# The order of the front stage: when the queries' weights are loaded, and what goes ahead of them

## The chip, the cores and the metric

The kernel runs on one core of a Trainium2 chip. A core has five engines that run their own instruction queues in order: TensorE (PE: matmuls, with weight loads shown as PEld), VectorE (DVE), ScalarE (ACT), GpSimd (POOL) and SyncE (SP). In this kernel SP does nothing but issue DMAs, plain ones and transposing ones; the bytes are moved by 16 DMA engines. The engines meet through semaphores.

The metric is the device time of one execution in microseconds (us). Before the change the median of three runs is 395.75 us (395.14 to 397.88).

## The reference

One transformer block over 2048 tokens of width 576, in bfloat16: a pre-norm linear attention ("hedgehog") and a pre-norm MLP, each with its residual.

```
h  = x + A(layernorm(x))          A: qkv = y @ wqkv, 32 heads of 18
h2 = h + B(layernorm(h))          B: layernorm, gelu(y @ w1 + b1) @ w2 + b2, 4608 hidden

phi(t)  = concat(softmax(t @ w_phi), softmax(-(t @ w_phi)))      per head, t = q or k
kv      = sum over tokens of phi(k) v^T,   z = sum of phi(k)
o       = phi(q) kv / (phi(q) z + 1e-6),   then o @ wo
```

No softmax over tokens is taken, so the keys of all tokens must be through before the first query can be combined with `kv`.

## The kernel before

**Tiles.** The 2048 tokens lie as 16 tiles of 128; two tiles make a *pair* p = 0..7, and `i` or `a` = 0, 1 names one tile of it (in `stats`, `centre`, `scale`, `sums`), or a half of the 32 heads (in `key_mm`, `key_exp`, `key_sum`, `value_mm`, `value_ev`). Each pair goes through: `stats` (mean and variance, VectorE), `power` (the inverse root, GpSimd), `scale` (the normalised rows, into one of three buffers `lnb`, number p % 3), a turn (the transpose, so that features lie on partitions), `key_mm` and `value_mm` (TensorE), `key_exp` (ScalarE, two exponentials), `key_sum` (VectorE: the softmax's sums and their inverse), `key_weigh` (GpSimd: the product with the inverse, a quarter of a pair each), and `sums` (TensorE, accumulates `kv`).

**A scale on one engine or the other.** VectorE subtracts the mean and multiplies in one instruction. ScalarE multiplies and adds a bias, and the bias, -mean times the inverse root, is first made by GpSimd in `centre`:

```
if eng is act:
    shifted(dst, src, rs, moments[p][2 + i], i)
else:
    eng.tensor_scalar(dst, src, mv[:, i, 0:1], rs[:, i : i + 1], ALU.subtract, ALU.mult)
```

**A turn.** Pairs 0 and 1 are transposed by TensorE (`turn_x_mm`, `turn_x_ev`); all others by `turn_dma` (L315), one transposing DMA on SP's queue from `lnb` (a region of the tile `shared`) into the pair's `home`.

**The weights.** `w_phi` is folded into the projections: the key weights are transposed by TensorE and folded at the start (`flip`, `fold_k`). The query weights go another way: `load_wq` (L598) brings them in by five DMAs, one for each 128 rows, each row in five pieces of 126 columns; `turn_wq(c)` (L368) transposes chunk c by DMA into `wT`; `fold_mm("q", c)` (L393) multiplies it with `w_phi`; `fold_ev` writes it to `wqp`, and `swap_q` copies halves of it between partitions. `load_wo(half)` (L604) brings in the output projection, 648 KB a half; it is first needed by `residual_mm`, after the attention.

**Banks.** The blocks of `key_mm`, `value_mm`, `query_mm` and of the folds share three PSUM tiles in turn (`two`), so a block can start only when the third block before it has been read, mostly by ScalarE.

**The order.** The program is written as a flat list of such calls, and nothing reorders it: each engine executes its instructions in the order in which the list names them. SP's queue before the change, from the start to the 40th microsecond, is

```
load_wk x3, load_x(2, 4), load_x(4, 8), load_values x4, load_x(8, 12), load_wq,
turn_dma(2), turn_wq(4), load_wo(0), turn_wq(1), turn_dma(3), turn_wq(2),
turn_wq(3), turn_wq(0), turn_dma(4), load_x(12, 16), turn_dma(5)
```

TensorE's blocks in the same stretch: keys of pair 0, values and keys of 0 and 1 mixed, keys of pair 2, `value_mm(1, 0)`, `sums(0, 0)`, `value_mm(2, 0)`, `key_mm(1, 1)`, `value_mm(2, 1)`, then `key_mm(3, 0)`, `value_mm(3, 0)`, `key_mm(3, 1)`, `sums(0, 1)`, `value_mm(3, 1)`, `fold_mm("q", 0)`, and the rest of the folds among the pairs 4 and 5. The queries follow from about 50 us, the combination with `kv` and the output projection from about 75 us, and from 90 us to the end the MLP, with the combination of the later pairs in between.

Of the kernel before, what the change touches and what calls it, by code (L numbers as in the profile page):

```python
# [43 lines left out]
def kernel(  # L44
# [213 lines left out]
    def shift(mv, rs, i):  # L258
        nb = small.tile([P, 1], FP32, name="nb", tag="nb", bufs=6)
        nc.gpsimd.tensor_scalar(  # L260
            nb[:, :], mv[:, i, 0:1], rs[:, i : i + 1], -1.0, ALU.mult, ALU.mult
        )
        return nb

    def shifted(dst, src, rs, nb, i):
        nc.scalar.activation(  # L266
            dst, src, AF.Identity, bias=nb[:, :], scale=rs[:, i : i + 1]
        )

    def chunks(t):  # L270
        return xh[:, t, :].rearrange("p (c k) -> p c k", k=KH)
# [6 lines left out]
    def turned(p):  # L278
        return lnT[p // 2][:, p % 2, :, :]

    def stats(p, i):
        if i == 0:
            moments[p] = [small.tile([P, 2, 2], FP32, name="mv", tag="mv")]
        mv = moments[p][0]
        st = small.tile([P, 2, nc.vector.BN_STATS_DIM], FP32, name="st", tag="st")
        for h in range(2):
            nc.vector.bn_stats(st[:, h, :], xh[:, 2 * p + i, h * HALF : (h + 1) * HALF])
        nc.vector.bn_aggr(mv[:, i, :], st[:, :, :])
        if i:
            moments[p] = [mv, None, None, None]  # L290

    def power(p):
        va = small.tile([P, 2], FP32, name="va", tag="va")
        nc.gpsimd.tensor_scalar(va[:, :], moments[p][0][:, :, 1], 1.0, EPS, ALU.mult, ALU.add)
        rs = small.tile([P, 2], FP32, name="rs", tag="rs")
        nc.gpsimd.tensor_tensor(rs[:, :], va[:, :], mhalf[:, 0:2], ALU.pow)
        moments[p][1] = rs

    def centre(p, i):
        moments[p][2 + i] = shift(*moments[p][:2], i)  # L300

    def scale(p, i, eng):
        mv, rs = moments[p][:2]
        dst, src = lnb[p % 3][:, :, i, :], chunks(2 * p + i)
# [3 lines that stand above are left out]
            eng.tensor_scalar(  # L308
                dst, src, mv[:, i, 0:1], rs[:, i : i + 1], ALU.subtract, ALU.mult
            )  # L310

    pool, vec, syn, sca = nc.gpsimd, nc.vector, nc.sync, nc.scalar

    def turn_dma(p):
        nc.sync.dma_start_transpose(  # L315
            turned(p), lnb[p % 3][:, :, :, :].rearrange("p c a k -> p (c a k)")
        )

    act, dve, gps = nc.scalar.copy, nc.vector.tensor_copy, nc.gpsimd.tensor_copy
# [22 lines left out]
    def turn_x_ev(p, part, copy):  # L342
        turned_back(("x", p), turned(p), part, copy)
# [23 lines left out]
    def turn_wq(c):  # L367
        nc.sync.dma_start_transpose(wT[:, :, c * P : (c + 1) * P], wq[:, c, :])  # L368
# [3 lines left out]
    def fold_k_mm(c):  # L372
        flight["k", c] = two.tile([P, 2, 512], FP32, name="pW", tag="two")[:, :, :]
        for g in range(NG):
            k = P if g < NG - 1 else 72
            for a in range(2):
                nc.tensor.matmul(
                    folded_part(g, "k", c, slice(a * KH, (a + 1) * KH)),
                    wT[:k, g, c * KH : (c + 1) * KH],
                    bd[:k, g, 0 : GH[g], :].rearrange("p h f -> p (h f)"),  # L380
                    start=True, stop=True,
                )

    def fold_k_ev(c, copy):
        fold_order.append(c)
        copy(wkp[:, c, :], folded_whole("k", c, P))  # L386
# [30 lines left out]
    def project(dst, lhs, w, i, order):  # L417
        for n, pick in enumerate(order):
            for a in range(2):
                rows = slice(a * KH, (a + 1) * KH)  # L420
                c = pick[a]
                slot = pick[0] if order is CROSSED else c
                nc.tensor.matmul(  # L423
                    dst[:, a, 0:HALF], lhs[rows, c, :], w[rows, slot, i * HALF : (i + 1) * HALF],
                    start=(n == 0), stop=(n == KC - 1),
                )

    def value_mm(p, i):
        pv = flight["v", p, i] = two.tile([P, 2, 512], FP32, name="pv", tag="two")
        project(pv, turned(p), wv, i, PLAIN)  # L430

    def value_ev(p, i, copy):
        copy(
            vals[:, 2 * p : 2 * p + 2, i * HH : (i + 1) * HH, 0:DH],
            flight["v", p, i][:, :, 0:HALF].rearrange("p a (h d) -> p a h d", d=DH),
        )
# [5 lines left out]
    def exponentials(key, dst, p, i):  # L442
        rows = dst[:, :, :].rearrange("p a (h s f) -> p a h s f", s=2, f=DH)
        for s in range(2):
            nc.scalar.activation(  # L445
                rows[:, :, i * HH : (i + 1) * HH, s, :],
                flight[key, p, i][:, :, 0:HALF].rearrange("p a (h f) -> p a h f", f=DH),
                AF.Exp, scale=1.0 - 2.0 * s,
            )
# [3 lines left out]
    def key_mm(p, i):  # L453
        features("k", wkp, p, i, PLAIN if p or i else [(c, c) for c in fold_order])

    def key_exp(p, i):
        if p not in phik:
            phik[p] = exk_pool.tile([P, 2, PW], BF16, name="phik", tag="exk")
        exponentials("k", phik[p], p, i)
# [12 lines left out]
    def total(key, dst, p, i):  # L472
        sk = small.tile([P, 2, NH], FP32, name="sk", tag="sk", bufs=6)
        nc.vector.tensor_reduce(sk[:, :, :], part_of(dst, i), AX.X, ALU.add)  # L474
        rk = flight["r" + key, p, i] = small.tile([P, 2, NH], FP32, name="rk", tag="rk", bufs=6)
        nc.vector.reciprocal(rk[:, :, :], sk[:, :, :])  # L476

    def weigh(key, dst, p, i, a, eng):
        part = part_of(dst, i)[:, a, :, :]
        eng.tensor_tensor(  # L480
            part, part,
            flight["r" + key, p, i][:, a, :].rearrange("p (h o) -> p h o", o=1).to_broadcast(
                [P, NH, DH]
            ),
            ALU.mult,
        )

    def key_sum(p, i):
        total("k", phik[p], p, i)

    def key_weigh(p, i, a, eng):
        weigh("k", phik[p], p, i, a, eng)
# [101 lines left out]
    def load_wq():  # L594
        for c in range(NC):
            m = P if c < NC - 1 else 64
            src = A_wqkv[c * P : c * P + m, 0 : NG * 126]
            nc.sync.dma_start(  # L598
                wq[:m, c, :].rearrange("p (g f) -> p g f", g=NG)[:, :, 0:126],
                src.rearrange("p (g f) -> p g f", g=NG),  # L600
            )

    def load_wo(half):
        nc.sync.dma_start(  # L604
            wo[half * KH : (half + 1) * KH, :, :],
            A_wo.rearrange("(k c) f -> k c f", c=KC),
        )
# [215 lines left out]
    fold_k_ev(2, act)  # L823
    fold_k_mm(6)
    fold_k_mm(5)
    load_wq()
    fold_k_ev(6, act)
    turn_x_mm(1)
    fold_k_ev(5, act)
    stats(2, 1)  # L830
    power(2)
    centre(2, 1)
    turn_x_ev(1, 0, dve)
    turn_x_ev(1, 1, dve)
    key_mm(0, 0)
    key_mm(0, 1)
    key_exp(0, 0)
    scale(2, 0, vec)
    scale(2, 1, act)
    turn_dma(2)  # L840
    stats(3, 0)
    stats(3, 1)
    stats(4, 0)
    stats(4, 1)
    value_mm(0, 0)
    power(3)
    key_sum(0, 0)
    key_exp(0, 1)
    value_ev(0, 0, act)
    turn_wq(4)  # L850
    load_wo(0)
    key_mm(1, 0)
    key_exp(1, 0)
    key_sum(0, 1)
    value_mm(0, 1)
    value_ev(0, 1, act)
    centre(3, 0)
    power(4)
    scale(3, 0, act)
    key_weigh(0, 0, 1, pool)  # L860
    key_weigh(0, 0, 0, pool)
    value_mm(1, 1)
    value_ev(1, 1, act)
    key_mm(2, 0)
    key_mm(2, 1)
    stats(5, 0)
    value_mm(1, 0)
    key_weigh(0, 1, 0, pool)
    scale(3, 1, vec)
    key_weigh(0, 1, 1, pool)  # L870
    sums(0, 0)
    key_exp(2, 0)
    key_exp(2, 1)
    stats(5, 1)
    power(5)
    value_ev(1, 0, act)
    key_sum(2, 0)
    key_weigh(2, 0, 1, pool)
    scale(4, 1, vec)
    value_mm(2, 0)  # L880
    value_ev(2, 0, act)
# [1 line left out]
    key_exp(1, 1)  # L883
    turn_wq(1)
    key_sum(2, 1)
    turn_dma(3)
    turn_wq(2)
    scale(4, 0, vec)
    centre(5, 1)
# [37 lines left out]
    key_sum(3, 0)  # L927
    key_weigh(3, 1, 0, pool)
    turn_dma(5)
    value_mm(4, 1)  # L930
    value_ev(4, 1, act)
    fold_mm("q", 1)
# [368 lines left out]
```

## Time and profile before

| | |
|---|---|
| median of the runs | 395.75 us (395.14 to 397.88, 3 runs) |
| the profiled execution: its time, its span | 397.2 us, 395.5 us |
| mean granted clock of TensorE | 0.995 |
| TensorE busy | 384.4 us, 97% of the span |
| VectorE, ScalarE, GpSimd busy | 165.0, 162.5, 120.9 us (42%, 41%, 31%) |
| VectorE busy from 22 to 34 us | 11.7 of 12 us |
| `turn_dma` from issue to landing, shortest, median, longest of six | 3.1, 4.2, 7.1 us |
| `load_wq` from issue to landing, the same of five | 3.8, 10.9, 12.4 us |

The span runs from the first instruction to the last, and the time of the execution has 1.7 us around it. Shares over the whole span say little of one stage: VectorE is at 42% of the span, but nearly full in the first 35 us. In a row of a timeline the first number is the start in us from the span's start, the second how long the group took; in brackets stands how long the engine was idle before it, and what released it. A row of waits gives the total, how often, and the longest. DMA rows give the issue on SP's queue; the landing is told separately.

### The profile page before, as it was taken

How to read it: one execution, taken by the hardware profiler on the slowest of the kernel's cores; microseconds unless marked ns; L12 is line 12 of the kernel's file. 1: busy time of each engine (PE TensorE's matmuls, PEld its weight loads, DVE VectorE, ACT ScalarE, POOL GpSimd, SP SyncE). 2: the span in 40 equal slices, each digit the busy share in tenths (PEclk: the TensorE clock that was granted, in tenths of full speed). 3: DMA queues.
4: the chain of work that ended last, by engine and by line, in shares of the span. 5: the costliest groups of instructions: out<-in, count | busy, mean ns of one | idle time of the engine just before them, and what ended most of it. 6: DMA issues, size and time to landing. Idle time of an engine off the chain costs nothing.

```text
span 395.5 us, 10241 instructions
## 1 busy us (share of the span) xinstructions
PE 384.4 (97%) x4492; PEld 267.3 (68%) x4493; DVE 165.0 (42%) x370; ACT 162.5 (41%) x288; POOL 120.9 (31%) x161
## 2 busy tenths in 40 slices
PE   8977999999999999999999999999999999999997
PEld 4855777779978887854447888444577864447873
DVE  6895987478039667682009333000390000000100
ACT  4865888668800770036660000566500016662000
POOL 7378799514504346226001211000032110000120
PEclk9998999999999999999999999999999999999999
DMA  8999449999953657543004372000042000000000
GB/s 230 211 161 189 100 93 193 203 264 341 249 111 75 122 96 143 76 76 73 2 2 62 75 120 46 17 1 2 2 88 62 17 17 0 2 2 0 17 25 22
DMA packets 75084, 35.43 MB, mean 90 GB/s; under 512 B 63026, under 2 KB 72384, under 8 KB 74912
## 3 DMA queue, kind: packets, MB, share of 16 engines
q1 hardware_dynamic: 74352, 33.14, 40.4%
q0 software_dynamic: 400, 1.35, 1.2%
q8 instruction: 35, 0.57, 0.6%
q10 hardware_dynamic: 288, 0.30, 0.2%
q14 instruction: 9, 0.07, 0.1%
HBM read 17.20 MB, written 2.36 MB: 49 GB/s over the span
## 4 chain that ended last, share of the span: by engine, by line
PE 90%; ACT 3%; DMA 3%; DVE 2%; POOL 1%; issue 1%; POOLq 0%
PE po L1185 36%; PE ph L1141 36%; PE pk L423 7%; PE pa L693 5%; PE pv L423 3%; DMA home<-shared 3%; PE acc_kv L559 1%; PE pn L644 1%; ACT shared L386 1%; ACT phik L445 1%; DVE ob L658 0%; PE pW L393 0%; ACT shared L266 0%; DVE shared L254 0%; PE pT L332 0%
## 5 line engine op out<-in xcount | busy, mean ns | idle before, releaser
L1163 ACT ACTIVATE home<-ph,b1col 128x512 bf16<-128x512 f32 (+1 forms) x180 | 98.6, 599 | 169.5 <-PE ph L1141 166.2
L1185 PE MATMUL po<-w,home 128*128 128x288 bf16 (+2 forms) x1151 | 143.2, 286 | 0.1
L1141 PE MATMUL ph<-shared,w 64*128 64x512 bf16 (+2 forms) x1638 | 141.3, 331 | 0.1
L1185 PEld LDWEIGHTS <-home 128*128 128x128 bf16 x1152 | 109.3, 98 | 32.1 <-issue 1.8
L1141 PEld LDWEIGHTS <-w 64*128 64x128 bf16 x1638 | 80.2, 94 | 60.1 <-issue 1.0
L1189 DVE TENSOR_TENSOR ot<-po,hb 128x288 bf16<-128x288 f32 (+2 forms) x32 | 14.5, 454 | 106.8 <-PE po L1185 100.9
L423 PEld LDWEIGHTS <-home 64*128 64x128 bf16 x864 | 42.4, 96 | 16.5 <-DMA home<-shared 5.5
L1174 POOL TENSOR_TENSOR hb<-xh,b2bc 128x576 f32<-128x576 bf16 x16 | 20.4, 1273 | 104.6 <-DVE ot L1189 102.8
L509 POOL TENSOR_TENSOR padded<-home,rq 128x540 bf16<-128x540 bf16 x32 | 34.8, 1103 | 37.0 <-DVE rq L501 14.9
L702 DVE TENSOR_TENSOR xh<-pa,xh 128x288 bf16<-128x288 f32 x32 | 13.2, 448 | 71.7 <-PE pa L693 71.7
L250 POOL TENSOR_TENSOR rs<-va,mhalf 128x1 f32<-128x1 f32 x16 | 8.8, 550 | 104.3 <-DVE va L248 104.3
L480 POOL TENSOR_TENSOR phik<-phik,rk 128x576 bf16<-128x576 bf16 x32 | 36.4, 1165 | 6.0 <-DVE rk L476 5.2
L423 PE MATMUL pk<-shared,home 64*128 64x288 bf16 x288 | 20.6, 291 | 4.8 <-DMA home<-shared 4.6
L474 DVE TENSOR_REDUCE sk<-phik 128x64 f32<-128x1152 bf16 x16 | 21.2, 1323 | 8.0 <-ACT phik L445 7.9
L445 ACT ACTIVATE phik<-pk 128x576 bf16<-128x576 f32 x32 | 18.9, 654 | 9.6 <-PE pk L423 9.6
L445 ACT ACTIVATE home<-pk 128x576 bf16<-128x576 f32 x32 | 18.9, 650 | 6.7 <-PE pk L423 5.5
L423 PE MATMUL pv<-wv,home 64*128 64x288 bf16 x288 | 21.0, 291 | 0.0
L500 DVE TENSOR_REDUCE sk<-home 128x64 f32<-128x1152 bf16 x16 | 21.0, 1313 | 0.0
L423 PE MATMUL pk<-wqp,home 64*128 64x288 bf16 x288 | 19.8, 283 | 0.2 <-ACT home L445 0.2
L657 DVE RECIPROCAL rec<-pn 128x18 f32<-128x18 f32 (+1 forms) x32 | 8.0, 249 | 27.9 <-PE pn L644 27.9
L693 PE MATMUL pa<-wo,shared 64*128 64x288 bf16 x288 | 18.8, 283 | 0.0
L693 PEld LDWEIGHTS <-shared 64*128 64x128 bf16 x288 | 13.9, 94 | 4.3 <-issue 0.5
(78 smaller groups left out, 201.3 us busy)
## 6 DMA issues: line engine op xcount, KB each, us to landing
w<-in_B_w_dram SPq DMA_DIRECT2D x21, 432.0 KB, 7.6
out_dram<-ot SPq DMA_DIRECT2D x15, 144.0 KB, 1.9
xh<-in_A_x_dram SPq DMA_DIRECT2D x3, 576.0 KB, 9.7
wo<-in_A_wo_dram SPq DMA_DIRECT2D x2, 648.0 KB, 7.3
w<-in_B_w_dram POOLq DMA_DIRECT2D x3, 432.0 KB, 10.6
wv<-in_A_wqkv_dram SPq DMA_DIRECT2D x2, 360.0 KB, 8.5
w<-in_A_wqkv_dram SPq DMA_DIRECT2D x4, 157.5 KB, 11.6
wv<-in_A_wqkv_dram SPq DMA_DIRECT2D x2, 288.0 KB, 9.6
```

The source lines that it names most:

```text
L423: nc.tensor.matmul(dst[:, a, 0:HALF], lhs[rows, c, :], w[rows, slot, i * HALF : (i + 1) * HALF], start=(n == 0), stop=(n == KC - 1),)
L445: nc.scalar.activation(rows[:, :, i * HH : (i + 1) * HH, s, :], flight[key, p, i][:, :, 0:HALF].rearrange("p a (h f) -> p a h f", f=DH), A ...
L474: nc.vector.tensor_reduce(sk[:, :, :], part_of(dst, i), AX.X, ALU.add)
L480: eng.tensor_tensor(part, part, flight["r" + key, p, i][:, a, :].rearrange("p (h o) -> p h o", o=1).to_broadcast([P, NH, DH]), ALU.mult,)
L500: nc.vector.tensor_reduce(sk[:, :, :], part_of(phiq[p], i), AX.X, ALU.add)
L509: eng.tensor_tensor(padded[:, a, g0 * P : (g0 + 5) * P].rearrange("p (g k) -> p g k", k=P)[:, :, 0:STEP].rearrange("p g (h f) -> p g h f", ...
L693: nc.tensor.matmul(pa[a], oT[p % 2][rows, c, :], wo[rows, c, cs], start=(c == 0), stop=(c == KC - 1),)
L1141: nc.tensor.matmul(ph[half][:, lo:hi], w1[p_ // 9][rows, c, p_ % 9 * P : (p_ % 9 + 1) * P], ln2T[rows, c, base + lo : base + hi], start=(c ...
L1163: nc.scalar.activation(hidden(m), ph[half][:, 0:width], AF.Gelu_apprx_tanh, bias=b1col[:, m : m + 1], scale=1.0,)
L1174: nc.gpsimd.tensor_tensor(hb[:, :], xh[:, t, :], b2bc[:, :], ALU.add)
L1185: nc.tensor.matmul(po[:, :], hidden(m)[:, i_ * P : (i_ + 1) * P], w2[m // 18][:, m % 18, cs], start=(j == 0), stop=(j == NM - 1),)
L1189: nc.vector.tensor_tensor(ot[:, cs], po[:, :], hb[:, cs], ALU.add)
```

## The change

The list of calls is reordered between 12 and 45 us; the instructions stay the same, but for one scale that changes its engine.

- `load_wq` goes from before `turn_dma(2)` to right behind it on SP's queue.
- The second tile of pair 2 is scaled by VectorE instead of ScalarE, and its `centre` on GpSimd falls away.
- Pair 3 goes ahead: `power(3)`, `centre(3, 0)`, both its scales, and `turn_dma(3)`, which now stands right behind `load_wq` and ahead of all five `turn_wq`. Its scale of tile 0 stands on ScalarE behind `key_exp(1, 0)`, that of tile 1 on VectorE behind `key_sum(0, 0)`.
- `stats` and `power` of pairs 4 and 5 go later: those of 4 behind `key_sum(0, 1)`, those of 5 behind `key_sum(2, 0)`.
- `load_wo(0)` goes from behind `turn_wq(4)` to behind `turn_dma(5)`.

TensorE's own order is not touched.

```diff
     fold_k_mm(5)
-    load_wq()
     fold_k_ev(6, act)
     ...
     power(2)
-    centre(2, 1)
     turn_x_ev(1, 0, dve)
     ...
     scale(2, 0, vec)
-    scale(2, 1, act)
+    scale(2, 1, vec)
     turn_dma(2)
+    load_wq()
     stats(3, 0)
     stats(3, 1)
-    stats(4, 0)
-    stats(4, 1)
+    power(3)
     value_mm(0, 0)
-    power(3)
     key_sum(0, 0)
     key_exp(0, 1)
     value_ev(0, 0, act)
-    turn_wq(4)
-    load_wo(0)
+    centre(3, 0)
+    scale(3, 1, vec)
     key_mm(1, 0)
     key_exp(1, 0)
+    scale(3, 0, act)
+    turn_dma(3)
+    turn_wq(4)
     key_sum(0, 1)
     value_mm(0, 1)
     value_ev(0, 1, act)
-    centre(3, 0)
-    power(4)
-    scale(3, 0, act)
     key_weigh(0, 0, 1, pool)
     key_weigh(0, 0, 0, pool)
+    stats(4, 0)
+    stats(4, 1)
     value_mm(1, 1)
     value_ev(1, 1, act)
     key_mm(2, 0)
     key_mm(2, 1)
-    stats(5, 0)
+    key_weigh(0, 1, 0, pool)
+    key_weigh(0, 1, 1, pool)
+    power(4)
     value_mm(1, 0)
-    key_weigh(0, 1, 0, pool)
-    scale(3, 1, vec)
-    key_weigh(0, 1, 1, pool)
     sums(0, 0)
     key_exp(2, 0)
     key_exp(2, 1)
-    stats(5, 1)
-    power(5)
     value_ev(1, 0, act)
     key_sum(2, 0)
     key_weigh(2, 0, 1, pool)
+    stats(5, 0)
+    stats(5, 1)
+    power(5)
     scale(4, 1, vec)
     ...
     turn_wq(1)
     key_sum(2, 1)
-    turn_dma(3)
     turn_wq(2)
     ...
     turn_dma(5)
+    load_wo(0)
     value_mm(4, 1)
```

## The prediction

> **What bounds the kernel now.** I read the page first, then TensorE's waits, the chain of work that ended last, the windows of 2 us around its DMA pieces, and the timelines of the queues. The page names the full engine, the waits its holes.
>
> ```profile
> PE 384.4 (97%) x4492; PEld 267.3 (68%) x4493; DVE 165.0 (42%) x370; ACT 162.5 (41%) x288; POOL 120.9 (31%) x161
> ...
> PE pk L423 <- DMA home<-shared: 4.6, 2, 2.4
> ```
>
> TensorE works 97% of the span, so an edit that leaves its work and its order alone can only close holes. One row holds nearly all of them: two waits, 4.6 us, for a transposing DMA from `shared` to `home`, a `turn_dma`. The chain (start, us, what) shows both:
>
> ```profile
> 19.37 4.06 DMA home<-shared
> ...
> 23.48 1.29 PE pk L423 x18
> 24.80 1.19 ACT phik L445 x2
> 25.99 7.12 DMA home<-shared
> ...
> 33.15 2.16 PE pk L423 x18
> ```
>
> The first is the third pair, p = 2, issued at 19.37 and landed at 23.43; the second is the fourth pair, issued at 25.99 and landed 7.12 us later. After the second, 18 matmuls take 2.16 us instead of 1.29. The windows (busy time of PE, PEld, DVE, ACT, POOL, then granted clock, DMA share, GB/s) say why:
>
> ```profile
> 12.00:14.00 2.00, 1.56 (x37) 1.30 (x37) 2.00 (x5) 2.00 (x5) 0.13 (x1) 1.00 1.13 241
> ...
> 22.00:24.00 2.00, 0.52 (x10) 0.42 (x12) 1.93 (x4) 0.23 (x1) 1.16 (x2) 1.00 0.51 108
> ...
> 32.00:34.00 2.00, 0.85 (x10) 0.61 (x12) 1.97 (x3) 0.21 (x1) 2.00 (x3) 0.85 0.74 156
> 34.00:36.00 2.00, 2.00 (x20) 1.29 (x18) 1.32 (x3) 0.65 (x2) 2.00 (x3) 0.50 1.16 212
> 36.00:38.00 2.00, 2.00 (x30) 1.45 (x26) 0.00 (x0) 1.19 (x3) 2.00 (x2) 0.80 0.96 308
> ```
>
> The clock falls to half after the second hole, not after the first: 2 x (0.15 + 0.50 + 0.20) = 1.7 us of lost clock. So 4.6 + 1.7 = 6.3 us hang on these two transposes. SP's queue says what they stood behind (start, us of issue):
>
> ```profile
> 7.09 12.16 SPq L598 DMA_DIRECT2D w<-in_A_wqkv_dram  x5
> 19.37 2.41 SPq L315 DMA_TRANSPOSE home<-shared  x1
> 22.54 1.20 SPq L368 DMA_TRANSPOSE w<-w  x1
> 23.79 0.59 SPq L604 DMA_DIRECT2D wo<-in_A_wo_dram  x1
> ...
> 27.66 4.87 SPq L368 DMA_TRANSPOSE w<-w  x3
> 32.63 1.32 SPq L315 DMA_TRANSPOSE home<-shared  x1
> ```
>
> `load_wq` holds SP from 7.09 to 19.25, and `turn_dma(2)` goes right after it. The 7.12 us of `turn_dma(3)` had wo's first half and a `turn_wq` before it on the queue.
>
> **The change part by part.** No matmul changes place on TensorE, so I follow every queue from 15 us on, with start-to-start durations from these rows.
>
> ```profile
> 15.62 0.57 DVE L308 TENSOR_SCALAR shared<-xh,mv,rs 128x576 bf16<-128x576 bf16 x1 [0.41 <-POOL rs L296]
> 16.11 0.81 DVE L287 BATCH_NORM_STATS2 st<-xh 128x6 f32<-128x288 bf16 x2
> ...
> 18.91 0.82 DVE L287 BATCH_NORM_STATS2 st<-xh 128x6 f32<-128x288 bf16 x2 [0.82 <-DMA xh<-in_A_x_dram]
> ...
> 20.81 1.30 DVE L474 TENSOR_REDUCE sk<-phik 128x64 f32<-128x1152 bf16 x1
> ...
> 22.61 1.29 DVE L474 TENSOR_REDUCE sk<-phik 128x64 f32<-128x1152 bf16 x1
> ...
> 34.88 0.47 DVE L308 TENSOR_SCALAR shared<-xh,mv,rs 128x576 bf16<-128x576 bf16 x1
> 39.57 1.35 DVE L474 TENSOR_REDUCE sk<-phik 128x64 f32<-128x1152 bf16 x1 [4.22 <-ACT phik L445]
> ```
>
> VectorE: a scale costs 0.49 (15.62 to 16.11), one `stats` 0.95 (two from 18.91 to 20.81), a `key_sum` 1.80 (20.81 to 22.61).
>
> ```profile
> 15.76 1.19 ACT L445 ACTIVATE phik<-pk 128x576 bf16<-128x576 f32 x2 [1.37 <-PE pk L423]
> 16.84 0.87 ACT L266 ACTIVATE shared<-xh,nb,rs 128x576 bf16<-128x576 bf16 x1
> 17.59 1.19 ACT L445 ACTIVATE phik<-pk 128x576 bf16<-128x576 f32 x2
> 18.66 0.66 ACT L433 CAST vals<-pv 128x576 bf16<-128x576 f32 x1
> ...
> 18.17 0.19 POOL L294 TENSOR_SCALAR va<-mv 128x2 f32<-128x2 f32 x1 [2.22 <-DVE mv L288]
> ...
> 19.25 0.27 POOL L260 TENSOR_SCALAR nb<-mv,rs 128x1 f32<-128x1 f32 x1
> ...
> 22.84 4.53 POOL L480 TENSOR_TENSOR phik<-phik,rk 128x576 bf16<-128x576 bf16 x4 [0.89 <-DVE rk L476]
> ...
> 17.75 1.28 PE L423 MATMUL pk<-shared,home 64*128 64x288 bf16 x18
> 18.85 2.38 PE L423 MATMUL pv<-wv,home 64*128 64x288 bf16 x36
> ...
> 39.86 0.44 PE L393 MATMUL pW<-w 128*128 128x126 bf16 x5
> ```
>
> ScalarE: `key_exp` 1.1, a scale 0.75, `value_ev` 0.55 to 0.66. GpSimd: `power` 1.08, `centre` 0.27, a weigh 1.13. TensorE: 1.10 per block of 18, and ScalarE can read a block about 1.3 after its start (23.48 to 24.80 in the chain).
>
> *Third pair.* The scale of p = 2, i = 1 leaves ScalarE (-0.75, and GpSimd's `centre`) and costs VectorE 0.49: done at 15.62 + 0.49 + 0.5 = 16.6 instead of 17.7. With `load_wq` out of the way SP issues the turn at 16.7. Unladen it takes 1.32 us to issue. The landings (min/median/max, of `load_wq`, then `turn_dma`, then `turn_wq`):
>
> ```profile
> L598 SPq DMA_DIRECT2D w<-in_A_wqkv_dram x5: 385/1628/6020, 7.1 to 18.6; - x5
> DMA to landing us min/median/max: 3.8/10.9/12.4
> ...
> DMA to landing us min/median/max: 3.1/4.2/7.1
> ...
> DMA to landing us min/median/max: 4.0/5.4/6.3
> ```
>
> Landing: 16.7 + 3.1 to 4.2 = 19.8 to 20.9. TensorE is through with its two value blocks at 18.85 + 2 x 1.10 = 21.05. The first wait goes whole: the third pair's keys start at 21.06 instead of 23.48, **-2.42**. What is late next there is nothing: the stationary banks are free by 21.6, the weigh that `sums(0, 0)` needs by 24.0, against a start at 24.4.
>
> *`load_wq` behind it.* Its price on an idle DMA is not in the trace. Below: five times the shortest issue, 1.9 us. Above: the 12.16 of before. I take 3.3, near the low end (0.6 to 0.7 each, like wo's 0.59), since the 12.16 were spent with the DMA engines full (share 1.13 in the window at 12) of value and x loads that are landed by then. SP is free again at 18.1 + 3.3 = 21.4.
>
> *Fourth pair ahead.* VectorE goes on with two `stats` (to 18.5), `key_sum` (20.25), scale (3, 1) (20.7), and no longer waits 0.82 for x. GpSimd has `power(3)` and `centre(3, 0)` done at 19.95; ScalarE, with nothing of the second pair's scale, is through `key_exp(1, 0)` at 20.2 and scales (3, 0) by 21.0. Behind that scale stand two `value_ev`, which come 0.75 later than they could; their banks are asked for at 22.2, 0.6 after they are free, so this costs nothing. `turn_dma(3)` goes at 21.4 and lands 3.1 to 7.1 later; I take 4.5 (wq's last packets before it, wo gone): 25.9. TensorE, after six blocks of 1.10 and one `sums` of 0.4 from 21.06 on, asks at 28.1 (before: 23.48 + 7.1 = 30.6, then 2.5 of wait). The keys start at 28.1 instead of 33.15: **-2.63** beyond the first term.
>
> *The clock.* From 33.15 to 39.86 before, four blocks and one `sums` took 6.7; at 1.10 and 0.4 they take 4.8: **-1.9**, of which the windows show 1.7 as clock. The Trainium skill, "TensorE: Matmul & The Clock Gate", section "What's actually happening", says that the clock drops only after an idle window of about 3.4 us, and that windows run free of the kernel. By the length alone neither hole here would do it; the 0.50 after a hole of 2.37 shows that it does, and the 1.00 after one of 2.25 that it need not. By its free-running window the term would be there in some executions and absent in others, which makes it a rival below.
>
> *A new wait.* `stats(5)` moves behind `key_sum(2, 0)`: VectorE at 24.35, 26.15, then two `stats` to 28.1; GpSimd's `power(5)` and `centre(5, 1)` to 29.5; ScalarE's scale (5, 1) stands until then, and behind it `value_ev(2, 1)`, done at 31.0 instead of 29.0. Its bank is what `key_mm(3, 1)` takes, wanted at 30.2: **+0.8**. Before, the hole at 33 covered it.
>
> *`turn_wq` later.* All five now stand behind `turn_dma(3)` (SP free at 22.8), and the first waits for wq's last part: issued at 20.8, landed 3.8 later, 24.6. Five issues of 1.2 (row) to 1.62 (4.87 / 3): the last starts between 29.4 and 31.1 and lands 4.0 to 5.4 later, 33.4 to 36.5. `fold_mm("q", 0)` wants it at 28.1 + 4.8 + 0.8 = 33.7. I take 34.4, near the short end because wo no longer runs among them: **+0.7**. `turn_dma(4)` follows it on SP at about 31 and lands at 35; the fourth value block asks at 35.9. Cover just suffices.
>
> *wo's first half* leaves the place where it delayed the transposes (counted above) and goes behind `turn_dma(5)`, about 36.5. What is queued behind it are the swaps of wqp; those wait for the last folds anyway. No row of TensorE waits for wo or wqp: 0, at most +0.8.
>
> *VectorE and GpSimd* do the same work as before. VectorE's first stretch ends 0.82 - 0.49 = 0.33 earlier, at about 34.9, and it then starts the `key_sum` that it started at 39.57: 4.7 earlier at most, since the hole of 4.22 is all the slack there is. Up to here TensorE is 2.42 + 2.63 + 1.9 - 0.8 - 0.7 = 5.45 earlier. What it has beyond 4.7 it is likely to lose again, waiting for weighed keys: **+0.7**. Afterwards all moves together, and the stages from 90 us on hold no wait for a DMA.
>
> **Sum: -4.7 us.** The profiled execution took 397.2 (span 395.5 and 1.7 around it), which becomes 392.5; the median of the runs is 395.75, 1.45 lower, and I put the same difference on it: **391.0**. One per cent, 4.0 us, is about what a measurement of this kernel can tell from no change.
>
> **The rivals.** (1) *The transposes of wq become the bound.* At the long end (36.5) TensorE waits 2.1 us more than I took, and `turn_dma(4)` comes as late: -2.6, 393.1. For it: five issues in a row on one queue, one of them waiting for a landing. Against: wo is gone from among them. (2) *The half clock is not in the median execution*, or comes back after one of the new waits: without 1.9, capped by nothing, -3.5, 392.3. For it: of two like holes one did it. (3) *The change doesn't do what it says*: `turn_dma(3)`, now behind `load_wq`, lands at 30 to 32; the first term stays, the second shrinks and the clock may fall: -1 to -2, 394.2. (4) *Slower:* `load_wq` holds SP for its 12.16 again, this time in front of the fourth turn. SP free at 30.3, turn landed at 33.4 (before 33.11), five `turn_wq` from 31.6, the last at 38.1, landed 4.7 later at 42.8; the fold that ran at 39.86 runs 2.9 later, and the long hole costs up to 1.7 of clock: 398.7 to 400.4. It decides from about 9 us of issue, where the last `turn_wq` lands at 39.9. Against it: the rings are empty of the large loads.
>
> The Trainium skill, "DMA: Bandwidth & Descriptors", section "Queues, rings and completion order", has descriptors of one issuing engine consumed in ring order on each DMA engine, which speaks against putting the fourth turn behind wq; the 7.12 behind wo against 3.1 agrees. By it the turn would land when wq has drained; that is rival (3).
>
> **How the numbers follow.** Forecast 0.50; (1) 0.18; (2) 0.13; (3) 0.10; (4) 0.09. The forecast's own range is 389.4 (no new wait: -6.3) to 392. The range of 8 in 10 takes in (1), (2) and most of (3): 389.3 to 394.6. Faster by over 1% is below 391.8: most of the forecast, a third of (2) and some of (1), 0.53; slower by over 1%, above 399.7, is the far end of (4), 0.04; the rest 0.43.
>
> **What would show it.** In the profile after: `turn_dma(2)` issued near 16.7, no wait of TensorE at its keys; the five loads of wq taking 3 to 4 us of SP, not 12; the fourth turn landed before 28; a granted clock of 1.00 from 20 to 40; a ScalarE hole before scale (5, 1) near 29; the first q fold near 34; VectorE's hole of 4.22 mostly gone. The prediction is wrong if the issue of `load_wq` is long, if a `turn_wq` lands after 36, or if TensorE waits for GpSimd's weighs between 40 and 75 by more than 1 us.

## The result, and the profile after

The kernel after takes 394.95 us (median of 20 runs, 393.5 to 396.5), the kernel before 396.26 beside it (20 runs, 394.71 to 398.18): a ratio of 0.9963, 95% interval 0.9945 to 0.9981. The gain is 1.3 us, some 0.4 per cent, where 4.7 us were forecast. The profiled execution took 395.62 us (span 393.9, granted clock 1.00 throughout), against 397.2 (span 395.5).

The front of the kernel did nearly all that was forecast of it. SP's timeline of the kernel after (start, us of issue):

```profile
16.82 1.38 SPq L315 DMA_TRANSPOSE home<-shared  x1
18.25 3.94 SPq L598 DMA_DIRECT2D w<-in_A_wqkv_dram  x5
22.31 1.47 SPq L315 DMA_TRANSPOSE home<-shared  x1
24.73 7.40 SPq L368 DMA_TRANSPOSE w<-w  x5
32.18 1.36 SPq L315 DMA_TRANSPOSE home<-shared  x1
33.59 0.58 SPq L173 DMA_DIRECT2D xh<-in_A_x_dram  x1
34.99 1.24 SPq L315 DMA_TRANSPOSE home<-shared  x1
36.28 0.88 SPq L604 DMA_DIRECT2D wo<-in_A_wo_dram  x1
38.01 0.64 SPq L410 DMA_DIRECT2D wqp<-wqp  x1
...
40.11 0.49 SPq L408 DMA_DIRECT2D wqp<-wqp  x1
```

`turn_dma(2)` goes at 16.82, `load_wq` takes 3.94 us instead of 12.16, and the fourth pair's turn goes at 22.31, ahead of all five `turn_wq`. TensorE's timeline shows what came of it, and where it was lost again:

```profile
21.18 2.38 PE L423 MATMUL pk<-shared,home 64*128 64x288 bf16 x36
...
28.33 1.27 PE L423 MATMUL pk<-shared,home 64*128 64x288 bf16 x18
...
31.11 1.28 PE L423 MATMUL pk<-shared,home 64*128 64x288 bf16 x18 [0.42 <-ACT vals L433]
...
33.95 0.44 PE L393 MATMUL pW<-w 128*128 128x126 bf16 x5
...
43.79 0.48 PE L559 MATMUL acc_kv<-vals,phik 128*128 128x57 bf16 x11 [0.65 <-POOL phik L480]
...
47.88 0.77 PE L423 MATMUL pk<-wqp,home 64*128 64x288 bf16 x9 [1.80 <-DMA wqp<-wqp]
...
72.61 0.79 PE L644 MATMUL pn<-kvm,shared 128*128 128x57 bf16 x22
...
86.81 3.15 PE L1140 MATMUL ph<-shared,w 64*128 64x128 bf16 x72
...
90.69 14.91 PE L1140 MATMUL ph<-shared,w 64*128 64x256 bf16 x270 [0.73 <-ACT home L1162]
105.54 0.42 PE L1184 MATMUL po<-w,home 128*128 128x288 bf16 x2
```

The same marks in the timeline of before:

```profile
75.56 0.80 PE L644 MATMUL pn<-kvm,shared 128*128 128x57 bf16 x22
...
89.80 17.88 PE L1141 MATMUL ph<-shared,w 64*128 64x128 bf16 x342
107.61 0.42 PE L1185 MATMUL po<-w,home 128*128 128x288 bf16 x2
```

The first fold of q starts at 33.95 instead of 39.86, 5.91 us earlier. The combination of queries with keys (`pn`, L644) starts 2.95 earlier, the MLP 2.99, its second product 2.07, and the span ends 1.6 earlier. So half of the gain goes between 34 and 48 us, and a part of the rest in the MLP.

TensorE's waits name the places. Those for transposes of x are gone; in their stead stand these (total us, times, longest):

```profile
PE pk L423 <- DMA wqp<-wqp: 1.8, 1, 1.8
...
PE ph L1140 <- ACT home L1162: 0.7, 1, 0.7
PE acc_kv L559 <- POOL phik L480: 0.6, 1, 0.6
```

None of the three was there before. The 0.6 is a wait for a weighed key, and the row of VectorE, which feeds GpSimd, says what that one waited for:

```profile
34.84 1.34 DVE L474 TENSOR_REDUCE sk<-phik 128x64 f32<-128x1152 bf16 x1
36.22 0.55 DVE L476 RECIPROCAL rk<-sk 128x64 f32<-128x64 f32 x1
39.62 0.82 DVE L287 BATCH_NORM_STATS2 st<-xh 128x6 f32<-128x288 bf16 x2 [2.85 <-DMA xh<-in_A_x_dram]
```

The `key_sum` that VectorE started at 39.57 before now starts at 34.84. But from 36.8 to 39.6 VectorE stands before `stats(6)`, for the last quarter of x, `load_x(12, 16)`, so that `stats(6)` starts only 1.8 us earlier than before (41.43). SP issued that load at 33.59, behind the five `turn_wq` and `turn_dma(4)`; before, at 34.0, its landing was hidden by the wait for ScalarE at 39.57. And the wait of 1.8 is for the last swap of wqp, which stands behind wo on the queue. The DMA issues of after (count, KB, us to landing):

```profile
wqp<-wqp SPq DMA_DIRECT2D x1, 72.0 KB, 7.7
```

and of before:

```profile
wqp<-wqp SPq DMA_DIRECT2D x1, 72.0 KB, 3.7
```

This swap takes twice as long to land. Two windows of after (fields as in those of before) show a DMA share of 0.04 just before the five loads of wq are issued at 18.25, and of 2.00 where wo follows x ahead of the swaps. The share counts a packet whole in the window in which it starts, so it can pass 1. TensorE is at full clock in both:

```profile
16.00:18.00 2.00, 2.00 (x37) 1.86 (x35) 1.97 (x6) 2.00 (x4) 0.00 (x0) 1.00 0.04 16
...
36.00:38.00 2.00, 2.00 (x35) 1.43 (x31) 0.74 (x2) 1.68 (x3) 2.00 (x3) 1.00 2.00 255
```

### The profile page after: what moved, and what is told of

Its sections match the earlier page's. It is cut to its first block, busy times and chain, and to the rows that moved or that the text cites. A ratio compares the mean times of both kernels' runs of the same rounds, so it can differ in the third digit from the quotient of the medians.

```text
span 393.9 us, 10235 instructions
## 1 busy us (share of the span) xinstructions
PE 383.0 (97%) x4492; PEld 267.4 (68%) x4493; DVE 165.1 (42%) x371; ACT 161.8 (41%) x287; POOL 120.4 (31%) x160
## 4 chain that ended last, share of the span: by engine, by line
PE 82%; DVE 7%; DMA 4%; SPq 2%; POOL 2%; issue 1%; ACT 1%; POOLq 0%; DVEq 0%
PE po L1184 35%; PE ph L1140 32%; PE pk L423 5%; PE pa L693 5%; PE pv L423 2%; DVE st L287 2%; DMA wqp<-wqp 2%; DMA w<-in_B_w_dram 2%; SPq L545 2%; PE pn L644 1%; PE acc_kv L559 1%; POOL padded L509 1%; DVE sk L474 1%; DVE shared L308 1%; DVE mv L288 1%
## 5 line engine op out<-in xcount | busy, mean ns | idle before, releaser
L423 PE MATMUL pk<-shared,home 64*128 64x288 bf16 x288 | 19.7, 283 | 0.7 <-ACT vals L433 0.4
```

Source lines behind the costliest of these rows:

```text
L423: nc.tensor.matmul(dst[:, a, 0:HALF], lhs[rows, c, :], w[rows, slot, i * HALF : (i + 1) * HALF], start=(n == 0), stop=(n == KC - 1),)
```

## The experiments

The theories were these. **A**: two landings that the change left late, or made late, take the gain back: the last quarter of x (through VectorE and GpSimd), and wo's first half in front of the swaps of wqp. **B**: later stages take it whatever is gained ahead of them, above all the MLP, whose weights come at their own pace. In the last experiment a further theory, **C**, stands against A: each wait stands by itself, so that what the front gains or loses shows in full at the end. The ratio of each run is to the kernel before in the same session. As a common measure in single profiles I use the start of the combination (`pn`, L644; 75.56 before, 72.61 after).

**wo moved out of the way, far back.**

```diff
     turn_dma(5)
-    load_wo(0)
     ...
     value_mm(7, 0)
+    load_wo(0)
     load_wo(1)
```

> The changed kernel with wo's first half issued directly ahead of its second half (near 59 us) instead of behind the sixth pair's turn (36.3 us). Theory A (the gain of the front was lost to DMAs in the wrong place, and what is saved there is carried to the end): the swaps of wqp land near 45 instead of 47.9, TensorE's wait of 1.80 for wqp is gone, the combination that starts at 72.61 starts near 70.7, and the time falls by 1.8 to 2.0 us against the changed kernel (ratio to before about 0.992). Theory B (the stream of MLP weights that runs from 72 to 110 us sets the start of the MLP's second half, whatever the front does): the wait is gone and 72.61 becomes 70.7 as well, but TensorE loses it again between 87 and 115 us; the time falls by 0 to 0.5 us (ratio 0.995 to 0.996).

Measured: 402.77 us, ratio 1.0149 (1.0116 to 1.0182). The wait for wqp is gone, but TensorE has others:

```profile
PE acc_kv L559 <- POOL phik L480: 2.5, 2, 1.9
PE pn L644 <- DMA shared<-padded: 2.4, 1, 2.4
PE ph L1140 <- ACT home L1162: 1.7, 1, 1.7
```

Two things are seen. Without the wait for wqp the one for the weighed keys grows, from 0.6 to 2.5: the two stood side by side. And both halves of wo now stand at 61 us ahead of the first transposes of the queries, which land after 9.9 us instead of 6.8 before and become late by 2.4 us; `pn` starts at 77.64. That second part is the new place's own price. It isn't all of the loss: without it `pn` would start at 75.23, still 2.6 us later than in after, and this execution also has 3.4 us of half clock from 52.5 on and a wait of 0.73 for a turn. So this run says nothing against A, and nothing for it but the first part. The wait of the MLP's first product for ScalarE (1.7) is of the kind of the 0.7 in after.

**The last quarter of x early.**

```diff
     load_x(8, 12)
+    load_x(12, 16)
     ...
     fold_ev("q", 3, act)
-    load_x(12, 16)
```

> The changed kernel with the last quarter of x loaded right behind the third quarter (near 7 us) instead of behind the fifth pair's turn (33.6 us). Both theories: VectorE's wait of 2.85 for x at 39.6 is gone, the weighs of pair 3 come 2 to 3 us earlier, and TensorE's wait of 0.65 for them is gone; but the swaps of wqp still land at 47.9, so TensorE's wait for wqp grows from 1.80 to about 2.4 and the time stays (0.995 to 0.998). If VectorE's wait were the main loss, the combination would start 0.7 or more earlier than 72.61. The risk: the third pair's turn waits behind x, and TensorE waits up to 1 us near 21.

Measured: 393.98 us, 0.9938 (0.9904 to 0.9973). VectorE no longer stands before `stats(6)`, no wait for a weighed key is left, and that for the swaps has fallen too, since x's load no longer runs beside wo:

```profile
PE pk L423 <- DMA wqp<-wqp: 0.8, 1, 0.8
```

`pn` starts at 71.67, 3.89 before its time in the kernel before, and the second product of the MLP at 104.26, 3.35 before it. By B it would have stayed near the 105.54 of after.

**Both.** The edits of the last two together.

> Both moves: wo's first half near 59 us and the last quarter of x near 7 us. Theory A: both waits gone, the combination starts near 70.0 instead of 72.61, time 2.5 us below the changed kernel (ratio to before 0.989 to 0.991). Theory B: the combination starts near 70.0, but the end moves by at most 0.7 us (ratio 0.994 to 0.996), and TensorE's waits between 87 and 115 us grow by the difference.

Measured: 398.12 us, 1.0029 (1.0006 to 1.0051). SP's timeline, then TensorE's:

```profile
56.43 1.25 SPq L604 DMA_DIRECT2D wo<-in_A_wo_dram  x2
...
60.36 10.31 SPq L545 DMA_TRANSPOSE shared<-padded  x2
```

```profile
75.59 1.21 PE L644 MATMUL pn<-kvm,shared 128*128 128x57 bf16 x22 [5.31 <-DMA shared<-padded]
```

TensorE is at the combination at 75.59 - 5.31 = 70.28, 5.3 us ahead of before, and then waits 5.31 for the transposes behind wo, which land after 11.2 us. The gain is made and given back to another queue position. It took another place for wo to see it at the end (below).

**wo back to where it was.**

```diff
     turn_wq(4)
+    load_wo(0)
     ...
     turn_dma(5)
-    load_wo(0)
```

> The changed kernel with this one part undone: wo's first half back behind the first of the five transposes of wq. My prediction priced wo ahead of the transposes at about 3 us on the last of them: the last transposed chunk lands near 37 instead of before 34, the first q fold runs near 36.5 instead of 33.95 (+2.5), and the wait of 1.80 for wqp goes (-1.8): time within 1 us of the changed kernel, ratio 0.995 to 0.999. If the place of wo among the transposes costs nothing, the fold stays at 34 and the time falls by 1.8 us like that of the move to 59 us.

Measured: 397.68 us, 1.0024 (0.9999 to 1.0048), 2.7 us over the after's 394.95 of another session, or 0.6% by the ratios. Among the five `turn_wq` wo delays these, then a turn of x:

```profile
PE acc_kv L559 <- POOL phik L480: 1.9, 1, 1.9
PE pW L393 <- DMA w<-w: 1.8, 1, 1.8
...
PE pk L423 <- DMA home<-shared: 1.1, 1, 1.1
```

With the rest of the change and wo left in its old place there is no gain that can be measured: the front's gain is lost to these waits, 4.8 us of them, and `pn` starts at 75.05. This prices the old place, which the prediction had counted among the transposes of wq, not the new place that it put at "0, at most +0.8".

**wo behind the swaps; the same with x early; and both kernels once more.** Edits against after:

```diff
     turn_dma(5)
-    load_wo(0)
     ...
     swap_q(0)
+    load_wo(0)
     key_mm(4, 1)
```

> The changed kernel with wo's first half issued right behind the three swaps of wqp (near 41 us) instead of right ahead of them (36.3 us). If wo ahead of the swaps is what cost TensorE its 1.80: the swaps land near 44 to 45, that wait is gone (below 0.3), the combination starts at 70.6 to 70.9 instead of 72.61, and nothing new is in the way of the first query transposes, as it was with wo at 61 us: time 1.5 to 2.0 us below the changed kernel, ratio to before 0.991 to 0.993. If wo only passes the cost on to the next transfer in the queue: the seventh pair's turn (issued near 47) lands 2 us later and TensorE waits 1 to 2 us for it near 53; the time is that of the changed kernel, 0.996.

> The same, and the last quarter of x loaded behind the third quarter near 7 us. If the two transfers (wo ahead of the swaps, x behind the transposes) are the whole loss between 34 and 75 us: neither the wait for wqp nor that for GpSimd's weighs of pair 3, the combination starts near 70.2, and the time is 2.3 to 3 us below the changed kernel, ratio 0.988 to 0.991. If the MLP's weights bind the rest: 70.2 as well, but the ratio stays at 0.994 like that of x alone.

> The changed kernel once more, one look. If the waits in its profile belong to the order of the queues, they are all there again within 0.3 us: 0.65 for the weighs of pair 3, 1.80 for wqp, 0.73 in the MLP's first block, 0.32 for w2. If the two in the MLP are chance of one execution, they are gone or elsewhere, while the first two stay.

> The kernel before once more, one look. If the half clock after the second hole belongs to the hole, a stretch of 0.50 follows it again; if it depends on where the hole falls in a window that runs free of the kernel, it may be missing, or follow the first hole. The two waits for the transposes stay near 2.25 and 2.37 in both cases.

Measured, wo alone: 395.33 us, 0.9981 (0.9958 to 1.0003). The wait for wqp is gone (the swap lands in 4.0 us), and the forecast gain of 1.5 to 2.0 us doesn't come, because TensorE now stands as long for the keys:

```profile
49.11 0.65 PE L559 MATMUL acc_kv<-vals,phik 128*128 128x57 bf16 x17 [1.89 <-POOL phik L480]
49.69 4.05 PE L423 MATMUL pk<-wqp,home 64*128 64x288 bf16 x36
```

In this execution half clock follows that wait: 36 matmuls take 4.05 us instead of 2.38, and `pn` starts at 73.44, later than in after. By their mean clock 4 of the 12 runs have such a stretch (median 396.2 us); the other 8 have a median of 395.0.

With x early as well: 392.55 us, 0.9924 (0.99 to 0.9948), and neither wait is left:

```profile
52.63 1.28 PE L423 MATMUL pk<-shared,home 64*128 64x288 bf16 x18 [0.76 <-DMA home<-shared]
...
70.89 0.80 PE L644 MATMUL pn<-kvm,shared 128*128 128x57 bf16 x22
```

The one new wait of 0.76 is for `turn_dma(6)`, which now has wo ahead of it. On top of after, wo's move alone gains nothing that can be measured, since the wait for the keys takes the place of the other; x's alone is a little lower (0.9938 against 0.9963), as it shortens wo's wait too; both are lowest, 1.5 us below after by the ratios where 2.3 to 3 were forecast. By the ratios alone, with intervals of 0.2 to 0.35% to either side, these steps are small; the rows of the waits carry the argument. With both moves the first fold starts 5.6 us earlier than before (34.27), `pn` 4.7, and the span is 4.7 shorter. A holds.

The second profile of after (395.43 us, `pn` at 73.59) has the wait for wqp again, 1.75 us, and that for the keys, 0.64, but not the two in the MLP. Its first product runs through:

```profile
87.79 18.05 PE L1140 MATMUL ph<-shared,w 64*128 64x128 bf16 x342
```

So what the first profile of after lost in the MLP (0.73 here, some more at the weights of the second product) is not a lasting cost of the change. In the second profile the gain at `pn`, against that of before beside it (75.35), is 1.76 us, and 1.6 are left at the end. B falls: here, and in the run with wo behind the swaps and x early, the MLP carries what it is given; with x early alone it carries 3.3 of 3.9.

The second profile of before (396.99 us) shows two holes of 1.78 and 2.43 us, and half clock behind the longer one only:

```profile
34.00:36.00 2.00, 2.00 (x22) 1.28 (x18) 0.80 (x2) 1.20 (x2) 2.00 (x3) 0.52 1.19 214
36.00:38.00 2.00, 2.00 (x22) 1.21 (x18) 0.00 (x0) 0.64 (x1) 1.53 (x2) 0.62 1.09 284
```

**The two moves without the change** (before, with x early and wo behind the swaps).

```diff
     load_x(8, 12)
+    load_x(12, 16)
     ...
     turn_wq(4)
-    load_wo(0)
     ...
     fold_ev("q", 3, act)
-    load_x(12, 16)
     ...
     swap_q(0)
+    load_wo(0)
     key_mm(4, 1)
```

> The kernel before, with only the two transfers moved: the last quarter of x behind the third quarter, wo's first half behind the swaps of wqp; the front keeps its old order. If the gain of the changed kernel with both moves (0.9924) needs the new front, this one gains little: wo no longer stands before the fourth pair's turn, so that lands 2 to 3 us earlier and the second hole shrinks to 0 to 1 us, but x in front of wq delays the third pair's turn by 1 to 2 us: ratio 0.993 to 1.000. If the two moves alone make the gain, it is at 0.992 or below.

Measured: 396.29 us, 1.001 (0.9988 to 1.0032). The second hole goes, but with x's load ahead of `load_wq` the third turn is issued at 20.41 instead of 19.37; the first hole is longer, and the clock halves behind it (TensorE's timeline, then the windows):

```profile
24.48 3.98 PE L423 MATMUL pk<-shared,home 64*128 64x288 bf16 x36 [2.81 <-DMA home<-shared]
```

```profile
24.00:26.00 2.00, 1.52 (x14) 0.97 (x16) 1.90 (x7) 0.00 (x0) 2.00 (x3) 0.59 0.43 82
26.00:28.00 2.00, 2.00 (x22) 1.24 (x20) 0.38 (x2) 1.14 (x2) 1.77 (x3) 0.55 1.14 130
```

The two moves alone gain nothing that can be measured. What both together gain on top of the change needs the change's front.

**wo behind the sixth turn, x early.** Against after:

```diff
     load_x(8, 12)
+    load_x(12, 16)
     ...
     fold_ev("q", 3, act)
-    load_x(12, 16)
     ...
     turn_dma(5)
-    load_wo(0)
     ...
     turn_dma(6)
+    load_wo(0)
```

> The changed kernel with the last quarter of x early and wo's first half right behind the seventh pair's turn (near 48.5 us) instead of behind the swaps (41 us): the wait of 0.76 for that turn near 52.6 goes, the combination starts at 70.2 to 70.5 instead of 70.9, time 0.3 to 0.7 us below the kernel with wo behind the swaps, ratio 0.990 to 0.992. If wo then delays the eighth pair's turn, a wait of the same size stands there and the time is equal.

Measured: 392.09 us, 0.9908 (0.9884 to 0.9931), the lowest of all, 4.0 us under the 396.09 of before in the same session, though its interval overlaps that of wo behind the swaps with x early. wo goes at 49.06, where nothing behind it on SP is urgent, and TensorE reaches the combination 5.13 us before its time in the profile of before (SP's timeline, then TensorE's):

```profile
49.06 0.60 SPq L604 DMA_DIRECT2D wo<-in_A_wo_dram  x1
```

```profile
34.80 0.43 PE L393 MATMUL pW<-w 128*128 128x126 bf16 x5 [0.81 <-DMA w<-w]
...
70.43 0.80 PE L644 MATMUL pn<-kvm,shared 128*128 128x57 bf16 x22
```

None of the waits for wqp, weighed keys or turn 6 is left. A wait of 0.81 for a `turn_wq` is, the forecast's "`turn_wq` later" (+0.7). The first fold starts 5.06 us earlier than before, the combination and the second product of the MLP 5.13 (102.48), and the span is 5.1 shorter: with both landings out of the way all of the front's gain reaches the end.

**The fourth turn put back.** Against after, everything else kept:

```diff
     scale(3, 0, act)
-    turn_dma(3)
     turn_wq(4)
     ...
     key_sum(2, 1)
+    turn_dma(3)
     turn_wq(2)
```

> The changed kernel with one part undone: the fourth pair's turn back behind the second transpose of wq. It goes near 27.5 and lands near 31.5, so TensorE's second hole comes back with about 3 us. Theory A (what the front gains beyond some 3 us is lost again, because x and wqp land when the DMA queue lets them, whatever TensorE does): the waits of 0.65 and 1.80 shrink by as much, the combination starts within 0.7 us of 72.6, the time rises by at most 0.7 us, ratio 0.995 to 0.998, plus up to 1 us where the hole halves the clock. Theory C (each wait stands by itself): the later waits stay and the time rises by 3 us, ratio 1.003 to 1.005.

Measured: 396.3 us, 1.0018 (0.9998 to 1.0037), 0.55% above after by the ratios, some 2.2 us: without this one line nothing is left of the change's gain. TensorE's timeline, then the windows:

```profile
32.80 2.34 PE L423 MATMUL pk<-shared,home 64*128 64x288 bf16 x18 [3.96 <-DMA home<-shared]
```

```profile
32.00:34.00 2.00, 1.20 (x12) 0.76 (x14) 1.97 (x3) 0.00 (x0) 2.00 (x3) 0.50 0.62 120
34.00:36.00 2.00, 2.00 (x20) 1.28 (x18) 1.24 (x3) 0.82 (x2) 2.00 (x3) 0.50 0.76 145
```

A hole of 3.96 us and two whole windows of half clock come back, and the first fold starts at 40.27, 6.3 later than in after. But the waits for wqp and for the keys are gone (wo goes 5.8 us ahead of the first swap here, and the last one lands in 3.4 us), and the combination starts at 75.85, 3.2 later. So of 6.3 us at the front, half is lost to the later landings, and half is kept; against the second profile of after (first fold 34.61, combination 73.59) it is 5.7 and 2.3. This profiled execution is one of two among the 12 with two stretches of half clock (397.51 us, where the median is 396.3), so its rows show a larger loss than most. The price lies between what the theories A and C expect, and neither has it right.

## Why the prediction was wrong

The forecast was 391.0 us with a range of 389.3 to 394.6; 394.95 lies outside, above.

**Right: the front.** *Third pair*: keys at 21.18 (forecast 21.06), no wait, term -2.42 as given. *`load_wq`*: 3.94 us of issue for an estimate of 3.3. *Fourth pair*: landed before it was wanted, keys at 28.33 (28.1). *The new wait* behind scale (5, 1): 0.42 us (+0.8). *`turn_wq` later*: 0 in the first profile, 0.34 in the second, 0.81 in the best variant (+0.7). *The clock*: 1.00 in every window from 22 to 38. The first fold came at 33.95 (34.4); in the other profiles with this front and wo out of the transposes it lies between 33.86 and 34.95. Rivals (1), (3) and (4) are refuted by these rows: no transposes of wq that bound, a fourth turn that is early, and 3.94 us instead of the 9 from which (4) decides. The Trainium skill, "DMA: Bandwidth & Descriptors", section "Queues, rings and completion order", whose ring order was weighed there against the fourth turn behind wq, agrees more with what happened to the swaps of wqp. The last of them took 7.7 and 8.1 us to land where x and wo stood right ahead, 5.9 with wo alone, and 3.4 to 5.3 in the other profiles; no turn of x in after took more than 4.1.

**Wrong: "VectorE and GpSimd", +0.7.** The step took the hole of 4.22 as all the slack there is and closed it with the `key_sum` that follows. It didn't ask what that engine takes next. `stats(6)` needs the last quarter of x, and its landing is set by the load's place on SP's queue, not by VectorE: issued at 34.0 before and 33.59 after. The engine gained 4.7 us and stood 2.85 (3.69 in the second profile). What that costs TensorE is 1.9 when nothing else hides it (wo behind the swaps), so the term is about +1.9. The sign that the prediction gave for it, more than 1 us of waits for weighed keys, didn't show in the first profile (0.65), since the wait for wqp hid the rest.

**Wrong: "wo's first half", "0, at most +0.8".** What is queued behind wo was named, the swaps of wqp, and dismissed because they wait for the folds anyway. They do, but they then run into wo's 648 KB and the last of x: landing 7.7 us, a wait of 1.75 to 1.80. Since no row of before has TensorE wait for wqp, the step took its slack for unchanged, while the step itself gave the folds 5.9 us less of it. The two together cost TensorE 2.45 in the first profile (0.65 and 1.80), and the second partly hides the first: with both landings moved, the combination goes from 72.61 to 70.43, 2.2 us.

**Wrong: "Afterwards all moves together".** From 34 to 72 us it did not, by those waits. In the MLP it did in the second profile and in the two variants with both moves that gain; in the first profile of after a wait for ScalarE of 0.73 was in the way, as one of 1.7 was with wo far back, and no run shows their cause.

**The clock, -1.9: right in the profile, not in the median.** Rival (2) is borne out in part. In after all 20 executions have a mean granted clock of 0.999 or 1.000. By their mean granted clock, 52 of 75 executions of before in the three sessions of the experiments had at least one stretch of half rate, five of them two, and 23 none. In the first session the 8 at full clock have a median of 396.22 us and the 18 with one stretch (a mean of 0.995 or 0.996) one of 397.6; in the second it is 395.53 and 395.66, in the third 395.89 and 396.37. So the term is between nothing and 1.4 us in the median, and not settled by these runs. The Trainium skill, "TensorE: Matmul & The Clock Gate", section "What's actually happening", has windows that run free of the kernel; that the same holes halve the clock in some executions and not in others agrees with it. The idle window of 3.4 us that it asks for was not needed: holes of 1.89, 2.37, 2.43 and 2.81 us did.

Summed again with what was measured in the profile: 5.9 at the fold, less 2.45 for the two landings, less some 0.5 that no one wait carries, is the 2.95 at the combination; less what the MLP of that execution lost, the 1.6 of the span. The median gained 1.3, so 3.4 of the forecast 4.7 are missing. Taking both landings away brings back some 2.2 of them (0.9908 against 0.9963, and `pn` from 72.61 to 70.43). The cause of the other 1.2 stays open: the best variant is 5.1 us ahead of before in the profiles and 4.0 in the medians. That fits a term for the clock that the profile of before has in full and its median only in part, but no run tells this from other differences between executions.

## What to carry to other kernels

When a change makes an engine earlier, list what that engine takes next and where each of these comes from: a landing set by a place in an in-order queue doesn't move with the engine, and the old profile hides it under the wait that goes away. A large load has a price where small transfers or transposes that are needed soon are queued right behind it, so it belongs where the next of them is far off. And undoing one of two waits that lie side by side can show little or nothing; take both away before either is called harmless.

## What was not expected of the hardware

- Where 648 KB of wo stood right ahead of something that was needed soon, this was late: the last swap landed after 7.7 and 8.1 us with x beside wo and after 5.9 with wo alone, instead of 3.4 to 5.3, and with both halves ahead of the first transposes of the queries TensorE waited 2.4 and 5.3 us for those. Issued 5.8 us ahead of the first swap, wo delayed none (3.4).
- The same five loads of wq held SP for 12.16 us where they follow the loads of values and x (DMA share above 1 in the windows from 7 to 17 us of before), and for 3.94 where the DMA engines were idle just before them (0.04), with no change in the loads.
- The length of a hole of TensorE doesn't tell whether half clock follows. Holes of 1.89 (in two runs), 2.37, 2.43, 2.81 and 5.31 us came with 3.4 us of half clock, and one of 3.96 with 6.8 us of it; holes of 1.87, 2.25 and 2.41 came with none.
